# Four reorderings in a two-layer linear-attention and MLP kernel: rows before stores, output weights written later, a third tile turned earlier, statistics a tile ahead

## The chip, the core and the metric

The kernel runs on one core of one Trainium2 chip. Its engines work beside each other: TensorE (PE; loads of its weights are listed as PEld) multiplies matrices into PSUM, VectorE (DVE), ScalarE (ACT) and GpSimd (POOL) do what lies between, and SyncE (SP; its DMA queue is shown as SPq) asks for nearly all transfers between HBM and SBUF. The metric is device microseconds (us) of one execution. Before the change it is 2492.43 us, the median of three runs (2491.26 to 2493.83).

## What is computed

Two layers, each a Hedgehog linear attention (A) and an MLP with squared ReLU (B), all in float32, on 2048 rows of 576 numbers; there are 32 heads of 18 and 4608 hidden features.

```python
x = x + A(layernorm(x)); x = x + B(layernorm(x))      # twice, same weights
# A: q, k, v = heads(x @ wqkv)
#    phi(u) = concat(softmax(u @ w_phi), softmax(-u @ w_phi))
#    kv = phi_k^T v, z = sum over rows of phi_k
#    o  = (phi_q kv) / (phi_q z + 1e-6);  return merged(o) @ wo
# B: h = relu(x @ w1 + b1); return (h * h) @ w2 + b2
```

The sums kv and z run over all rows, so no row of a layer's attention output is known before every row's keys and values have been summed. This point is called the barrier.

## The kernel before

**Tiles.** The 2048 rows are four blocks of 512 (`NB`, `TB`); a block is four tiles of 128 rows (`NT`). The 576 columns are four chunks of 128 and a rest of 64 (`KC`, `NC` = 5). The turned features of a block come in five groups of heads (`NG`) in two halves of the feature map, so `2 * NG` = 10 steps. To keep precision, an operand of a matmul is split into a high part (ScalarE copies it) and a low part (VectorE or GpSimd subtracts), and a product is the sum of three: high by high, low by high, high by low. Weights once split are stored in HBM (`keep_split`, the stores at L406) and later loaded ready-made (L406 again).

**Order of work.** Layer 0 goes through the blocks in the order [3, 2, 0, 1], layer 1 in [1, 0, 3, 2]. In a layer: the barrier, with the attention output of order[0] (`g_out` with two parts and `pause`); the MLP of order[0] (`g_mlp`), into which the attention of order[1] is woven (`back_first`); the MLP of order[1], into which the attention of order[2] and order[3] is woven (`back_second`); then the MLP of the last two blocks as a pair (`g_pair`: `products` computes both blocks' hidden features and the first block's sums, `seconds` the second block's sums). Into layer 0's `seconds` the norms, values and keys of layer 1 are woven (`back_keys`).

**Who sets the order.** Python generators write the instructions down in one order: `weave(main, other, rate)` lets the other generator advance by the costs it yields, `pipeline` staggers stages over tiles. A scheduler then orders each engine's queue when the program is built: among what is ready by its own model, that which was written earlier goes first, unless `tc.issue_after` holds it behind a named instruction. Each engine, SyncE too, runs its queue strictly in that order, so an instruction that waits holds up all behind it. A load can be placed long before the place where it was written, if its buffer slot is free.

**The places that are touched.**
- The barrier, `g_out` with `pause`: the block's last two row tiles need their features scaled first: `product` (L828), `total` (sums, L831), `factors` (L797 to L800), `rescale` (L805), for halves 0 (VectorE) and 1 (GpSimd) of tiles 2 and 3. `between` writes them behind the first part's last eviction, with two `o_add` (L939), which add the first output products to the rows that `rows_in` loaded (L922). TensorE's transposes at L888 wait for the rescaled halves. `pieces` loads and splits the output weights, with GpSimd's low parts at L384.
- Without `behind`, in the blocks of order[2] and order[3], `pieces` loads the stored output weights: eight loads (L406), four of 567 KB and four of 81 KB.
- `last`, at the end of order[0]'s attention: transposes (L480, L494) and splits (ScalarE L488 and L501, VectorE L489 and L502) of the normalized tiles 2 and 3. `g_mlp` runs it (`drain(rest)`) behind the first half products (L1121) of its first two groups of features. A group's weights are loaded at L1091, L1093 and L238 and split at L1099 to L1106.
- `last_rows(0)` in `g_pair`: the last products are added to the rows of xm, in their last 128 columns at L1492, in the others at L1496, and the sum is stored to xs (L1498).
- `back_keys` and `g_norm` with `fine`: `start` loads a tile (L1742) and takes its statistics (L438, L441 on VectorE, L442 and L443 on GpSimd), `apart` normalizes it (L469, L470), `cross` transposes, `split` splits. The tag "x" has five slots, for the rows of `last_rows` and those of the norm.

Of the kernel before, what the change touches and what calls it, by code (L numbers as in the profile page):

```python
# [15 lines left out]
NT = TB // P  # L16
# [5 lines left out]
def layers_kernel(  # L22
# [18 lines left out]
    nc = tc.nc  # L41
# [10 lines left out]
    NC = KC + 1  # L52
    HG = P // DH
    GW = HG * DH
    NG = (H + HG - 1) // HG
# [24 lines left out]
    kept = set()  # L80
# [6 lines left out]
    spare = {"tags": [], "i": 0}  # L87
# [9 lines left out]
    def drain(gen):  # L97
        for _ in gen:
            pass
# [13 lines left out]
    def pipeline(n, stages, costs):  # L113

        for i in range(n + len(stages) - 1):
            for k in reversed(range(len(stages))):
                if 0 <= i - k < n:
                    stages[k](i - k)
                    yield costs[k]
# [36 lines left out]
    def lagged(n, produce, consume, by=1):  # L156

        held = {}
        for i in range(n + by):
            if i < n:  # L160
                held[i] = produce(i)
            if i >= by:
                consume(i - by, held.pop(i - by))
            if i < n or i == n + by - 1:
                yield
# [54 lines left out]
    dense = {"v": 0}  # L220
# [200 lines left out]
    def keep_split(which, pair):  # L421
        if which not in kept:
            for half in range(2):
                moved(which, half, pair[half], True)
            kept.add(which)
# [26 lines left out]
    def g_norm(x_of, dst, name, then=None, fine=False):  # L452
# [69 lines left out]
        xns, pts, begun = {}, {}, {}  # L522
# [16 lines left out]
            else:  # L539
                split_main(i // 3 * 2 + i % 3, pts.pop(i))  # L540

        yield from pipeline(NT, (start, apart), (2.0, 1.6))
        yield from pipeline(3 * NT // 2, (cross, split), (0.3, 0.9))

    def spill(b, x):
# [312 lines left out]
    def g_out(layer, b, ph, dst, name, parts=1, pause=None, behind=None, norm=None, mid=None, costs=(None, None)):  # L858
# [51 lines left out]
        def pieces():  # L910
            with ExitStack() as order:
                for ins in behind or ():
                    order.enter_context(tc.issue_after(ins.ins))
                if not pause or "o" in kept:
                    return wpair("o", name, low=nc.gpsimd if parts > 1 else None)
                two = [wpiece(wo, 0, f"{name}o0", heads=True, low=nc.gpsimd)]
            with tc.issue_after(late_products().ins):
                return two + [wpiece(wo, HP, f"{name}o1", heads=True, low=nc.gpsimd)]

        def rows_in(t):  # L920
            x = sb.tile([P, D], F32, tag="x", name=f"{name}x{t}", bufs=5)
            nc.sync.dma_start(x, x_in[b * TB + t * P : b * TB + (t + 1) * P] if layer == 0 else xs[b][t])  # L922
            return x
# [23 lines left out]
        if pause:  # L947
            product, total, factors, rescale = pause()
            with tc.issue_after(dense["scaled0"].ins):
                product(2, 0)  # L950
                total(2, 0)
        pair = pieces() if behind or "o" in kept else None
        if pair:
            keep_split("o", pair)
        if pause and not late:
            late_products()
        xs_of = []
        yield

        def between(pts):  # L960
            steps = [lambda: product(3, 0), lambda: total(2, 1), lambda: factors(2), lambda: rescale(2, 1),
                     lambda: total(3, 0), lambda: total(3, 1), lambda: factors(3), lambda: rescale(3, 1),
                     lambda: o_add(xs_of[0], pts[0], 0), lambda: o_add(xs_of[1], pts[1], 0),
                     lambda: rescale(2, 0), lambda: rescale(3, 0)]
            for step in steps:
                step()
                yield

        for part in range(parts):
            if pause and part:  # L970
                xs_of += [rows_in(t) for t in range(2)]
                pts = [o_product(t, half) for half in range(2) for t in range(2)]
                with tc.issue_after(dense["part"].ins):
                    drain(chained(between(pts), every=True))
            for i, _ in enumerate(lagged(2 * NG, lambda i: turn(part, i), lambda i, f: times(part, i, f), parts)):
                if pause and part and i in (1, 2):
                    with tc.issue_after(dense["turned"].ins):
                        o_add(xs_of[i - 1], pts[1 + i], 1)
                yield costs[0]
# [3 lines left out]
        pair = pair or pieces()  # L983
# [10 lines left out]
        begin, scale, main, rest = next(g_norm(xs_of.__getitem__, dst, f"{name}n", None, None))  # L994
        owns, xns, ox = {}, {}, {}
# [68 lines left out]

        def last():
            spare.update(tags=[f"acc{i}" for i in range(NC)], i=NC + 1)
            pts = [main[0](t, xns[t]) for t in (2, 3)]
            pts.append(rest[0](1))
            spare["tags"] = []
            yield  # L1070
            main[1](2, pts[0])
            main[1](3, pts[1])
            rest[1](1, pts[2])
            yield

        dense["rest"] = last()
# [2 lines left out]
    def g_mlp(layer, b, x, after, name, rest=None, then=None):  # L1079
# [3 lines left out]
        R = D - P  # L1083
# [76 lines left out]
        for f in range(2):  # L1160
            first(f, rest is not None)
            with tc.issue_after(traced_on(nc.tensor)) if rest else nullcontext():
                hidden(f, halves[0])
        if rest:
            with tc.issue_after(dense["hidden"].ins):
                drain(rest)
        acc += [ps_a.tile([P, TB], F32, tag=f"acc{c}", name=f"{name}acc{c}") for c in range(NC)]
        for low in lows:
            with tc.issue_after(dense["normed"].ins), tc.issue_after(dense["lowered"].ins):
# [187 lines left out]
    def g_pair(layer, blocks, x, after, name):  # L1357
# [120 lines left out]
        def last_rows(b):  # L1478
            f = (b + 1) * NF - 1
            features(f, range(3))  # L1480
            yt = sb.tile([P, TB], F32, tag="hr", name=f"{name}yt{b}", bufs=2)
            nc.scalar.activation(yt, accs[b][KC], AF.Copy)
            by_rows(f, range(2), range(3))
            pt = ps_w.tile([P, TB], F32, tag="w", name=f"{name}py{b}")
            p3 = pt.rearrange("p (t d) -> p t d", d=P)
            for t in range(NT):
                nc.tensor.transpose(p3[:, t], yt[:, t * P : (t + 1) * P], ident)
            xs_ = after if b else []
            for t in range(NT):
                xr = sb.tile([P, D], F32, tag="x", name=f"{name}x{b}{t}", bufs=5)  # L1490
                nc.sync.dma_start(xr, xm[blocks[b]][t])
                nc.vector.tensor_add(xr[:, R:], p3[:, t], xr[:, R:])  # L1492
                xs_.append(xr)
            by_rows(f, range(2, NT), range(3))
            for t, xr in enumerate(xs_):
                dense["added"] = nc.vector.tensor_add(xr[:, :R], accs[b][t][:, :R], xr[:, :R])  # L1496
                at = blocks[b] * TB + t * P
                nc.sync.dma_start(out[at : at + P] if layer else xs[blocks[b]][t], xr)  # L1498
            del high[f], wide[f]
# [221 lines left out]
    for layer in range(2):  # L1721
# [101 lines left out]
        for k, _ in enumerate(products):  # L1823
            if k == NP - 1:
                with tc.issue_after(dense["paired"].ins):
                    for _ in range(2):
                        next(back, None)
        with tc.issue_after(dense["added"].ins):
            for _ in range(4):
                next(back, None)  # L1830
        weave(seconds, back, 0.85)
        if layer == 0:

# [33 lines left out]
```

## Time and profile before

| | us |
|---|---|
| runs, median (lowest to highest) | 2492.43 (2491.26 to 2493.83) |
| profiled execution | 2491.15 |
| its span, first to last instruction | 2489.2 |
| TensorE busy | 2463.1 |
| VectorE busy | 1535.0 |
| ScalarE busy | 1263.0 |
| GpSimd busy | 956.7 |
| largest wait of TensorE (t0opt, L888) | 3.1 |

The clock granted to TensorE was 0.999 of full speed over the span. Tile names tell the place: t0 and t1 are the barriers of layers 0 and 1, a_2, a_0 and so on the attention of a block, m_3 and so on the MLP of a block, m_p the pair, n_3 a block's norm in `back_keys`, w_3v its value weights. In rows of the timeline the columns are the start in us, the length in us, the engine, line and operation, the tile written and the tiles read, shapes, the count of like instructions merged, and in brackets the idle time before with what ended it. Instructions of one engine overlap a little, so that lengths are somewhat above the distance between starts.

### The profile page before, as it was taken

To read this page: it belongs to the slowest core of one execution; us is meant where nothing else is said; L and a number is where in the kernel's file an instruction comes from. 1 tells how busy PE (TensorE), PEld (TensorE's weight loads), DVE (VectorE), ACT (ScalarE), POOL (GpSimd) and SP (SyncE) were. 2 spreads that over 40 slices of the span, in tenths; PEclk is the share of its full clock that TensorE was granted. 3 is DMA by queue.
4 is the path that set the end of the run, shared out by engine and by line. 5 is a ranking of instruction groups with operands and counts; after the bars stand their busy time and mean duration, and the time that the engine had idled before them with its cause. 6 is when DMAs were issued, how large, how long until landed. Compare 5 with 4: busy or idle time off the path is not lost. (4 is left out here: it accounts for less than half of the span.)

```text
span 2489.2 us, 41471 instructions
## 1 busy us (share of the span) xinstructions
PE 2463.1 (99%) x15108; PEld 2169.4 (87%) x15108; DVE 1535.0 (62%) x2507; ACT 1263.0 (51%) x2243; POOL 956.7 (38%) x1101
## 2 busy tenths in 40 slices
PE   8999999999999999999999999999999999999999
PEld 8998888889888888888999988888888888888888
DVE  7778938454756655545756787584557665454454
ACT  4344545443546766664443445554445466666543
POOL 4445303212335565541433442132122355565322
PEclk9999999999999999999999999999999999999999
DMA  9124533346434433338754144334473444333363
GB/s 332 60 71 146 169 105 94 103 156 224 131 120 134 146 104 105 110 100 287 250 196 144 54 169 116 103 99 117 153 243 96 125 136 139 115 104 112 108 200 127
DMA packets 248892, 348.67 MB, mean 140 GB/s; under 512 B 30127, under 2 KB 155951, under 8 KB 246127
## 3 DMA queue, kind: packets, MB, share of 16 engines
q1 hardware_dynamic: 247428, 344.66, 44.0%
q8 instruction: 118, 1.93, 0.3%
q10 hardware_dynamic: 1258, 1.37, 0.2%
q14 instruction: 88, 0.71, 0.1%
HBM read 280.93 MB, written 65.00 MB: 139 GB/s over the span
## 5 line engine op out<-in xcount | busy, mean ns | idle before, releaser
L1428 POOL TENSOR_TENSOR m_ps<-m_pr,m_ps 128x128 fp32r<-128x128 f32 x144 | 118.2, 821 | 310.9 <-ACT m_ps L1426 248.7
L1427 DVE TENSOR_TENSOR m_ps<-m_pr,m_ps 128x448 fp32r<-128x448 f32 x144 | 97.9, 680 | 166.1 <-ACT m_ps L1426 162.6
L1470 PE MATMUL m_pacc<-m_ps,m_phb 128*128 128x448 f32 x864 | 188.5, 366 | 0.0
L1470 PEld LDWEIGHTS m_pacc<-m_ps,m_phb 128*128 128x128 f32 x864 | 162.1, 188 | 18.2
L1426 ACT ACTIVATE m_ps<-m_pr 128x576 fp32r<-128x576 f32 x144 | 98.4, 683 | 128.1 <-issue 71.5
L1470 PE MATMUL m_pacacc<-m_ps,m_phc 128*128 128x448 f32 x648 | 150.3, 368 | 0.7 <-DVE m_px L1496 0.7
L1470 PEld LDWEIGHTS m_pacacc<-m_ps,m_phc 128*128 128x128 f32 x648 | 119.2, 188 | 10.0 <-DVE m_px L1496 1.0
L1148 PE MATMUL m_0acc<-m_0s,m_0hb 128*128 128x448 f32 x432 | 100.2, 366 | 0.0
L1148 PE MATMUL m_2acc<-m_2s,m_2hb 128*128 128x448 f32 x432 | 100.2, 366 | 0.0
L1148 PE MATMUL m_3acc<-m_3s,m_3hb 128*128 128x448 f32 x432 | 99.7, 365 | 0.0
L1148 PE MATMUL m_1acc<-m_1s,m_1hb 128*128 128x448 f32 x432 | 99.7, 365 | 0.0
L1121 PE MATMUL m_3ph<-t0onh,m_3h 128*128 128x512 f32 (+1 forms) x380 | 97.6, 382 | 0.6 <-ACT t0onh L488 0.5
L1121 PE MATMUL m_1ph<-t1onh,m_1h 128*128 128x512 f32 (+1 forms) x380 | 97.5, 382 | 0.6 <-ACT t1onh L488 0.5
L1121 PE MATMUL m_2ph<-a_2nh,m_2h 128*128 128x512 f32 (+1 forms) x380 | 97.7, 384 | 0.0
L1121 PE MATMUL m_0ph<-a_0nh,m_0h 128*128 128x512 f32 (+1 forms) x380 | 97.6, 384 | 0.0
L1148 PEld LDWEIGHTS m_2acc<-m_2s,m_2hb 128*128 128x128 f32 x432 | 80.9, 188 | 10.6 <-ACT m_2hb L1129 0.2
L1148 PEld LDWEIGHTS m_0acc<-m_0s,m_0hb 128*128 128x128 f32 x432 | 80.9, 188 | 10.6 <-ACT m_0hb L1129 0.2
L1148 PEld LDWEIGHTS m_1acc<-m_1s,m_1hb 128*128 128x128 f32 x432 | 81.1, 188 | 10.3
L1148 PEld LDWEIGHTS m_3acc<-m_3s,m_3hb 128*128 128x128 f32 x432 | 81.1, 188 | 10.3
L1106 POOL TENSOR_TENSOR m_3s<-m_3r,m_3s 128x128 fp32r<-128x128 f32 x36 | 24.6, 684 | 161.6 <-ACT m_3s L1100 148.1
L1106 POOL TENSOR_TENSOR m_1s<-m_1r,m_1s 128x128 fp32r<-128x128 f32 x36 | 24.2, 673 | 162.2 <-ACT m_1s L1100 154.8
L1106 POOL TENSOR_TENSOR m_0s<-m_0r,m_0s 128x128 fp32r<-128x128 f32 x36 | 28.1, 779 | 138.8 <-ACT m_0s L1100 131.1
(2439 smaller groups left out, 7341.3 us busy)
## 6 DMA issues: line engine op xcount, KB each, us to landing
m_pr<-in_B_w SPq DMA_DIRECT2D x144, 288.0 KB
m_pr<-in_B_w SPq DMA_DIRECT2D x72, 256.0 KB
hd<-m_pu SPq DMA_DIRECT2D x72, 256.0 KB
m_pg<-hd SPq DMA_DIRECT2D x72, 256.0 KB
m_3r<-in_B_w SPq DMA_DIRECT2D x36, 288.0 KB
m_2r<-in_B_w SPq DMA_DIRECT2D x36, 288.0 KB
m_1r<-in_B_w SPq DMA_DIRECT2D x36, 288.0 KB
m_0r<-in_B_w SPq DMA_DIRECT2D x36, 288.0 KB
```

The source lines that it names most:

```text
L1106: nc.gpsimd.tensor_sub(s2[:, D + R : 2 * D], r2[:, R:], s2[:, R:D].bitcast(F32))
L1121: dense["hidden"] = nc.tensor.matmul(ph[:, cols], a, m, start=(k == 0), stop=(k == len(ops) - 1))
L1148: nc.tensor.matmul(acc[t][:, :R], a[:, rows], m, start=(f == 0 and k == 0), stop=(f == NF - 1 and k == 2))
L1426: nc.scalar.activation(s2[:, :D], r2, AF.Copy)
L1427: nc.vector.tensor_sub(s2[:, D : D + R], r2[:, :R], s2[:, :R].bitcast(F32))
L1428: nc.gpsimd.tensor_sub(s2[:, D + R : 2 * D], r2[:, R:], s2[:, R:D].bitcast(F32))
L1470: nc.tensor.matmul(accs[b][t][:, :R], a[:, rows], m, start=(g == 0 and k == 0), stop=(g == NF - 1 and k == 2))
```

## The change

It has four edits, and adds or removes no arithmetic and no transfer.

1. In the barrier the first two row loads are written ahead of the stores of the split output weights (`keep_split("o", pair)`); before, these stores stood first and the rows were written at the start of the second part. The steps of `between` are reordered: `total(2, 1)`, `factors(2)` and `rescale(2, 1)` ahead of `product(3, 0)`, which was first.
2. In blocks without `behind` the output weights are loaded when half of the turned features are written (`i == NG`) instead of ahead of them all.
3. `last` is two steps: transposes and splits of tile 2, written behind the first half product of feature group 0, and those of tile 3 and of the rest, behind that of group 1. Before, both tiles and the rest were one step of transposes and one of splits, behind both half products.
4. In `g_norm` with `fine` a tile's statistics are written one tile ahead of the normalization of the one before. `back_keys` is advanced by one step, not two, behind the last product of the pair, and by one, not four, behind the adds of `last_rows(0)`. In `last_rows(0)` the four small adds (L1492) stand behind the four large ones.

```diff
@@ g_norm, fine
-        yield from pipeline(NT, (start, apart), (2.0, 1.6))
+        start(0)
+        yield 2.0
+        for t in range(NT):
+            if t + 1 < NT:
+                start(t + 1)
+                yield 2.0
+            apart(t)
+            yield 1.6
         yield from pipeline(3 * NT // 2, (cross, split), (0.3, 0.9))
@@ g_out
-        pair = pieces() if behind or "o" in kept else None
-        if pair:
-            keep_split("o", pair)
+        pair = pieces() if behind else None
         if pause and not late:
             late_products()
         xs_of = []
+        if pause:
+            xs_of += [rows_in(t) for t in range(2)]
+            keep_split("o", pair)
         yield
         def between(pts):
-            steps = [lambda: product(3, 0), lambda: total(2, 1), lambda: factors(2), lambda: rescale(2, 1),
+            steps = [lambda: total(2, 1), lambda: factors(2), lambda: rescale(2, 1), lambda: product(3, 0),
                      lambda: total(3, 0), lambda: total(3, 1), lambda: factors(3), lambda: rescale(3, 1),
...
             if pause and part:
-                xs_of += [rows_in(t) for t in range(2)]
                 pts = [o_product(t, half) for half in range(2) for t in range(2)]
...
             for i, _ in enumerate(lagged(2 * NG, lambda i: turn(part, i), lambda i, f: times(part, i, f), parts)):
+                if not behind and i == NG:
+                    pair = pieces()
@@ last
             spare.update(tags=[f"acc{i}" for i in range(NC)], i=NC + 1)
-            pts = [main[0](t, xns[t]) for t in (2, 3)]
-            pts.append(rest[0](1))
+            pt = main[0](2, xns[2])
             spare["tags"] = []
-            yield
-            main[1](2, pts[0])
-            main[1](3, pts[1])
-            rest[1](1, pts[2])
+            main[1](2, pt)
+            yield
+            spare.update(tags=[f"acc{i}" for i in range(NC)], i=NC + 2)
+            pt, pr = main[0](3, xns[3]), rest[0](1)
+            spare["tags"] = []
+            main[1](3, pt)
+            rest[1](1, pr)
             yield
@@ g_mlp, in the loop over the first two groups
-        if rest:
-            with tc.issue_after(dense["hidden"].ins):
-                drain(rest)
+            if rest:
+                with tc.issue_after(dense["hidden"].ins):
+                    next(rest)
@@ last_rows
-                nc.vector.tensor_add(xr[:, R:], p3[:, t], xr[:, R:])
+                if b:
+                    nc.vector.tensor_add(xr[:, R:], p3[:, t], xr[:, R:])
...
                 dense["added"] = nc.vector.tensor_add(xr[:, :R], accs[b][t][:, :R], xr[:, :R])
+            for t, xr in enumerate(xs_):
+                if not b:
+                    with tc.issue_after(dense["added"].ins):
+                        nc.vector.tensor_add(xr[:, R:], p3[:, t], xr[:, R:])
@@ layers_kernel
                 with tc.issue_after(dense["paired"].ins):
-                    for _ in range(2):
-                        next(back, None)
+                    next(back, None)
         with tc.issue_after(dense["added"].ins):
-            for _ in range(4):
-                next(back, None)
+            next(back, None)
```

## The prediction

> **What bounds the kernel now.** I read the profile page first for the span and the busy shares, then the table of waits of TensorE, longest first, then the timeline around each wait that a changed line can touch.
>
> ```profile
> span 2489.2 us, 41471 instructions
> PE 2463.1 (99%) x15108; PEld 2169.4 (87%) x15108; DVE 1535.0 (62%) x2507; ACT 1263.0 (51%) x2243; POOL 956.7 (38%) x1101
> ```
>
> TensorE is busy for 2463.1 of 2489.2 us. No matmul is added or removed, so the most that any reordering can win is the idle 26.1 us, 1% of the span; a loss has no such ceiling, since every wait put in front of TensorE adds to the end. The columns of the next rows are who waits, for whom, total us, times, longest.
>
> ```profile
> PE t0opt L888 <- DVE t0fQ2e L805: 3.1, 1, 3.1
> ...
> PE n_3p L494 <- DVE n_3l L489: 1.9, 1, 1.9
> PE a_3pn L904 <- DVE a_3fl L891: 1.8, 1, 1.8
> ...
> PE a_0pn L904 <- DVE a_0fl L891: 1.2, 1, 1.2
> PE m_pach L1470 <- DVE m_ps L1427: 0.9, 1, 0.9
> PE m_pacacc L1470 <- DVE m_px L1496: 0.7, 1, 0.7
> ```
>
> These six waits, 9.6 us together, are what the diff can reach: the barrier (3.1), the attention blocks of the second pair (1.2 in layer 0, 1.8 in layer 1), and the start of layer 1's norms (0.7, 0.9, 1.9). The profiled run took 2491.15 us, 1.95 outside the span, and lies 1.28 under the median of the runs, 2492.43. The sum below is made in us of the span and then taken from the median. About 0.2%, 5.0 us, is what a measurement of this kernel can tell from no change.
>
> **Part 1, rows ahead of the weights' stores, and the barrier's order.** VectorE in layer 0's barrier, then SyncE's queue, then GpSimd:
>
> ```profile
> 209.00 1.98 DVE L828 TENSOR_TENSOR t0fm<-t0fQ3e,zb 128x576 f32<-128x576 f32 x1
> ...
> 215.00 0.23 DVE L800 TENSOR_TENSOR t0fQ3r<-t0fQ3r,t0fu 128x64 f32<-128x64 f32 x1
> 216.16 0.46 DVE L939 TENSOR_TENSOR t0ox<-t0opo,t0ox 128x288 f32<-128x288 f32 x1 [0.94 <-DMA t0ox<-in_A_x]
> 217.71 0.46 DVE L939 TENSOR_TENSOR t0ox<-t0opo,t0ox 128x288 f32<-128x288 f32 x1 [1.09 <-DMA t0ox<-in_A_x]
> 218.09 0.75 DVE L805 TENSOR_TENSOR t0fQ2e<-t0fQ2e,t0fQ2r 128x576 f32<-128x576 f32 x1
> ```
>
> ```profile
> 210.38 1.57 SPq L406 DMA_DIRECT2D wsol<-t0oo1l  x2
> 212.04 1.78 SPq L922 DMA_DIRECT2D t0ox<-in_A_x  x4
> ```
>
> ```profile
> 207.67 3.96 POOL L384 TENSOR_TENSOR t0oo1l<-t0oo1r,t0oo1h 126x1152 fp32r<-126x1152 f32 x2
> ...
> 215.37 1.16 POOL L805 TENSOR_TENSOR t0fQ3e<-t0fQ3e,t0fQ3r 128x576 f32<-128x576 f32 x1 [1.29 <-DMA t0ox<-in_A_x]
> ```
>
> The last rescaling that TensorE waits for ends at 218.84. In front of it VectorE stands idle twice for the block's rows, 0.94 and 1.09 us, because SyncE asks for them at 212.04, behind stores (210.38) that wait for GpSimd's splits of 207.67. After the edit the rows are asked for ahead of those stores and are there by 215.23, when the factors end. Both gaps go, 2.03 us. What is late next is the rescaling itself: its start moves from 218.09 to 216.06, and there GpSimd still runs its own rescaling (215.37 to 216.53). Layer 1, which stores no weights, shows that order already:
>
> ```profile
> 1442.72 1.41 DVE L831 TENSOR_REDUCE t1fu<-t1fm 128x32 f32<-128x576 f32 x2
> ...
> 1445.91 1.56 DVE L805 TENSOR_TENSOR t1fQ2e<-t1fQ2e,t1fQ2r 128x576 f32<-128x576 f32 x1
> ```
>
> ```profile
> 1442.94 1.17 POOL L805 TENSOR_TENSOR t1fQ2e<-t1fQ2e,t1fQ2r 128x576 f32<-128x576 f32 x1 [7.35 <-DVE t1fQ2r L800]
> 1445.69 1.17 POOL L805 TENSOR_TENSOR t1fQ3e<-t1fQ3e,t1fQ3r 128x576 f32<-128x576 f32 x1 [1.58 <-DVE t1fQ3r L800]
> ```
>
> There the same rescaling took 1.56 instead of 0.75 beside GpSimd's. So 216.06 + 1.56 = 217.62 against 218.84: I take a gain of 1.2, of a possible 2.03, and at least 0. The product that moves behind the factors (1.98 beside the split) is the same work on the same engine; in layer 1 nothing in front of it is late, so I cost the reorder at 0. It could cost 1.17 in each layer, if it had to sit out GpSimd's rescaling of 1442.94, which then starts just ahead of it. I take 0 because the instruction behind the factors starts at 1442.72, before GpSimd's at 1442.94.
>
> The Trainium skill ("SBUF — State Buffer", section "Who interferes with whom") says that a VectorE instruction with two SBUF inputs and a GpSimd instruction that reads SBUF hold a shared port exclusively, whoever starts first. It speaks against the reorder, which puts two such instructions side by side; 1.56 against 0.75 agrees, and by it the sum would come out between the one above and 2.3 us less gain, according to who starts first.
>
> **Part 2, the output weights.** The eight loads of these weights are written behind the first half of the turned features in the blocks of order[2] and order[3]. SyncE's queue and ScalarE in layer 0, then the chain of waits in layer 1 (start, us, what), then the first use of these weights:
>
> ```profile
> 519.36 0.79 SPq L406 DMA_DIRECT2D a_0o1l<-wsol  x1
> 520.24 1.07 SPq L1093 DMA_DIRECT2D m_2r<-in_B_w  x2
> ...
> 523.87 0.40 SPq L922 DMA_DIRECT2D a_0x<-in_A_x  x1
> ```
>
> ```profile
> 525.97 0.69 ACT L1100 ACTIVATE m_2s<-m_2r 128x576 fp32r<-128x576 f32 x1 [2.10 <-DMA m_2r<-in_B_w]
> ```
>
> ```profile
> 1747.20 0.73 SPq L406
> ...
> 1748.03 6.36 DMA m_0r<-in_B_w
> ```
>
> ```profile
> 551.17 0.30 PE L933 MATMUL a_0po<-a_0o0h,a_0oh 126*128 126x288 f32 x1
> ```
>
> The MLP's weights are asked for at 520.24, behind the last piece of the output weights (519.36), and ScalarE's split of them (525.97, after a wait of 2.10) stands in front of the eviction for which TensorE waits 1.2. In layer 1 the same piece costs the queue 0.83 (1747.20 to 1748.03) before a transfer of 6.36. The pieces issued earlier found their slots free and the queue idle, and SyncE hoists such loads (at 523.87 it asks for a_0's rows, 27 us before the products of 551.17 that they are added to). So I expect the early pieces to stay and only the last to fall behind: 0.88 (520.24 less 519.36) plus its share of the transfers, about 0.35, covers the 1.2 of layer 0; and 0.83 + 0.35 = 1.2 of the 1.8 in layer 1. Together 2.4, with 0 and 3.0 as bounds. The weights then have until 551.17; order[3]'s have longer.
>
> **Part 3, the third tile turned sooner.** TensorE, then VectorE, as the MLP of order[0] starts:
>
> ```profile
> 236.53 0.85 PE L1121 MATMUL m_3ph<-t0onh,m_3h 128*128 128x256 f32 x5
> ...
> 239.95 1.04 PE L480 MATMUL t0onp<-ident,t0onn 128*128 128x128 f32 x8
> ...
> 241.72 1.68 PE L1121 MATMUL m_3ph<-t0onh,m_3h 128*128 128x256 f32 x9 [0.52 <-ACT t0onh L488]
> ```
>
> ```profile
> 238.09 0.49 DVE L469 TENSOR_SCALAR t0onn<-t0ox,t0onm,t0ond 128x512 f32<-128x512 f32 x1
> ...
> 242.54 0.43 DVE L502 TENSOR_TENSOR t0onh<-t0onp,t0onh 64x256 fp32r<-64x256 f32 x1
> ```
>
> Two half products take 3.42 us (236.53 to 239.95), 1.71 each. The third tile's transposes now follow the first, at 238.24; their input is ready at 238.58, so TensorE waits about 0.4 with the second half product queued behind. Its own eviction is then covered, but the fourth tile's transposes come some 0.4 later and the 0.52 wait behind them shrinks by about 0.3. Net loss 0.1 per layer, 0.2 in all, between a loss of 0.9 (the 0.4 not recovered) and a gain of 1.0 (the 0.52 gone in both).
>
> **Part 4, layer 0's last rows, and part 5, statistics a tile ahead.** VectorE, its waits between 1100 and 1170, SyncE's queue, and the DMA rows of 1143.5 to 1147.2:
>
> ```profile
> 1139.30 0.87 DVE L1492 TENSOR_TENSOR m_px<-m_ppy,m_px 128x128 f32<-128x128 f32 x4
> 1140.09 1.14 DVE L1496 TENSOR_TENSOR m_px<-m_pacc,m_px 128x448 f32<-128x448 f32 x2
> ...
> 1142.21 0.61 DVE L1427 TENSOR_TENSOR m_ps<-m_pr,m_ps 128x448 fp32r<-128x448 f32 x1
> ```
>
> ```profile
> DVE n_3n L469 <- POOL n_3d L443: 3.8, 4, 1.0
> ```
>
> ```profile
> 1142.41 1.13 SPq L1742 DMA_DIRECT2D x<-xs  x2
> ```
>
> ```profile
> DMA packets 437, 1.13 MB, mean 306 GB/s; under 512 B 48, under 2 KB 48, under 8 KB 436
> ...
> w_3v0h<-wsvh SPq DMA_DIRECT2D x1, 720.0 KB
> ```
>
> The four small adds (0.79 from start to start) move behind the two large ones, which free the accumulators 0.79 sooner: the 0.7 wait goes, gain 0.7 (0 to 0.8). The split of 1142.21 stands behind a tile's statistics that had waited for a load; with fewer steps of the norm forced ahead it no longer does: gain 0.8 of its 0.9 (0 to 0.9). The price: the next tile's row took the slot that the first tile's normalization freed. With statistics a tile ahead it needs a slot whose store has landed, as the loads of 1142.41 do, and that store is issued 0.79 later. I cost this at 0: the normalizations no longer each wait about 1.0 for GpSimd's root (3.8 in four), which pays back some 3 us of a load that has to wait for a store, and the transposes are written further down, behind more of the second products. The 1.9 wait at n_3p stays; bounds, it goes (gain 1.9) or grows as in rival A.
>
> The Trainium skill ("DMA: Bandwidth & Descriptors", section "Anatomy of one DMA") gives about 2.0 us plus bytes over 436 GB/s for a DMA. A store and a load of one row tile (128 x 576 numbers, 288 KB) would by it take an estimated 5.4 us, whatever lies before them; the rows here show a transfer of the same size at 6.36 behind others. No term of the sum rests on it.
>
> **Sum:** -1.2 - 2.4 + 0.2 - 0.7 - 0.8 = -4.9 us. The profiled time would be 2486.2, the median 2487.5.
>
> **The rivals.**
> A (can end on the other side): the late row. If the three loads of 720 KB of the value weights get ahead of the last row, 2.2 MB at the 306 GB/s of that stretch are 7 us more for n_3p to wait: -4.9 + 7 = +2.1. Where the 3 us of the roots' waits aren't won back either and the store's 0.79 counts, it is 10.8 and +5.9; it decides from 9.9 on. For it: 1142.41 is already behind a store. Against it: those weights are written behind the norm's sixth step.
> B (slower): the output weights arrive late. 576 x 576 numbers in a high and a low part are 2592 KB, at 306 GB/s 8.7 us, the first half 4.4; asked for later than 546.8, TensorE waits us for us in both layers. It decides from 551.8 on, where 2 x 5.0 eat the 4.9 and 5 more. Against it: the hoisting above.
> C: all loads really move, the rescaling starts clear of GpSimd, and n_3p's wait goes: -4.9 - 0.6 - 0.8 - 1.9 = -8.2.
> D: the loads and the rows keep their places: -4.9 + 1.2 + 2.4 = -1.3.
> E: the product loses to GpSimd's rescaling in both barriers: -4.9 + 2.3 = -2.6. That is the port rule's case.
>
> **How the numbers follow.** Forecast 0.40 (own range -7 to -2; faster by over 0.2% in 0.22, within it in 0.18), A 0.19 (within 0.09, slower 0.10), B 0.08 (slower), C 0.22 (faster), D 0.06 and E 0.05 (within). Faster 0.44, within 0.2% 0.38, slower 0.18. The range from -10.4 (2482) to +4.1 (2496.5) leaves out B, the worst of A and a little beyond C.
>
> **What would show it.** Right: no gap before the two adds of L939 in layer 0's barrier and t0opt's wait near 1.9; the load of L1093 ahead of the last a_0o1l and a_3o1l, and the waits of a_0pn and a_3pn gone and near 0.6; m_pacacc's and m_pach's waits gone; m_3ph's two waits about 0.6 together. Wrong: a row of L1742 landing after the value weights and n_3p's wait above 4; a_0po or a_3po in the table of waits; a new wait of 1 us or more anywhere else, since each such wait outweighs one term.

## The result, and the profile after

The changed kernel takes 2486.89 us, the median of 11 runs (2483.94 to 2488.61), against 2491.26 for the kernel before in the same comparison (11 runs, 2488.80 to 2493.83). The ratio is 0.9979, with a 95% interval from 0.9971 to 0.9988: 4.4 us between the two medians. A few executions of the experiments below took from 7% to several times longer, and their medians and ratios leave these out. The profiled execution took 2485.02, and its page begins:

```profile
span 2483.3 us, 41469 instructions
...
PE 2462.7 (99%) x15108; PEld 2169.3 (87%) x15108; DVE 1533.3 (62%) x2507; ACT 1262.7 (51%) x2243; POOL 959.9 (39%) x1101
```

TensorE's work is the same, 15108 matmuls; the span is 5.9 us shorter. So the difference lies in waits and pace, not in work. The table of TensorE's waits after the change (who, for whom, total us, times, longest; lines are some 7 to 16 higher than before):

```profile
PE k_3kp L571 <- DMA w_3k1l<-wskl: 1.5, 1, 1.5
PE t0opt L895 <- DVE t0fQ2e L812: 1.2, 1, 1.2
PE n_3p L480 <- DVE n_3n L469: 1.1, 1, 1.1
PE n_3p L494 <- DVE n_3l L489: 0.9, 2, 0.7
```

Gone altogether are a_0pn (1.2), a_3pn (1.8), m_pach (0.9) and m_pacacc (0.7); t0opt fell by 1.9. The norm n_3 waits 2.0 in three places instead of 1.9 in one. New is k_3kp: TensorE stands 1.5 us for the last piece of the key weights. Together -6.5 + 0.1 + 1.5 = -4.9 in the table; of the rest of the 5.9, 0.5 is the first wait for DMA (fp, 2.5 before and 2.0 here), which reads 2.0 to 3.3 in the profiles of this study.

Waits are not all that TensorE loses. Behind the wait of t0opt the kernel before ran on at a lower granted clock. The four microseconds from TensorE's restart, here and in the kernel with the rows and the barrier changed alone (below); the columns are the stretch, its length, the busy us and the number of instructions of PE, PEld, DVE, ACT and POOL, the granted clock, the DMA share and GB/s:

```profile
218.90:222.90 4.00, 3.72 (x19) 3.27 (x20) 2.75 (x7) 1.95 (x6) 0.62 (x1) 0.68 0.03 8
```

```profile
218.30:222.30 4.00, 3.68 (x25) 3.00 (x26) 3.16 (x9) 2.99 (x8) 0.96 (x1) 1.00 0.01 4
```

The clock record of the kernel before reads 0.5 for 3.41 us from 220.3 on. From the restart to the last product of the barrier the same matmuls take 17.2 to 17.5 us in the seven profiles that have such a stretch there, and 16.3 to 16.4 in the seven without: 1.1 us that count as busy and stand in no row of waits.

**The barrier.** VectorE, then SyncE's queue, after the change:

```profile
209.12 0.64 DVE L804 TENSOR_TENSOR t0fu<-t0fu,t0fQ2r 128x64 f32<-128x64 f32 x1
209.80 0.70 DVE L805 SCALAR_TENSOR_TENSOR t0fu<-t0fu 128x32 f32<-128x32 f32 x1
...
211.06 0.75 DVE L835 TENSOR_TENSOR t0fm<-t0fQ3e,zb 128x576 f32<-128x576 f32 x1
...
214.31 0.82 DVE L946 TENSOR_TENSOR t0ox<-t0opo,t0ox 128x288 f32<-128x288 f32 x2
215.04 1.27 DVE L812 TENSOR_TENSOR t0fQ2e<-t0fQ2e,t0fQ2r 128x576 f32<-128x576 f32 x1
```

```profile
203.94 1.27 SPq L929 DMA_DIRECT2D t0ox<-in_A_x  x2
```

The rows are asked for at 203.94, and the two adds follow the factors without a gap. The rescaling now takes 1.27 instead of 0.75: it stands beside GpSimd's, as forecast. The product takes 0.75 instead of 1.98, since GpSimd's split is over (at 210.44) when it comes; the small factors in front of it pay part of that (0.64 and 0.70, against 0.23 and 0.19 before). The product starts 0.23 us ahead of GpSimd's rescaling (211.06 against 211.29, and in layer 1 1438.00 against 1438.23), keeps its 0.75 in both layers, and GpSimd's takes 1.55 instead of 1.17.

**The output weights.** SyncE's queue in layer 0:

```profile
511.35 0.36 SPq L1104 DMA_DIRECT2D m_2r<-in_B_w  x1
511.75 1.21 SPq L406 DMA_DIRECT2D a_0o1h<-wsoh  x1
514.32 2.42 SPq L1215 DMA_DIRECT2D xs<-m_3x  x4
516.84 0.91 SPq L1104 DMA_DIRECT2D m_2r<-in_B_w  x1
517.81 0.69 SPq L406 DMA_DIRECT2D a_0o1h<-wsoh  x1
518.54 0.84 SPq L406 DMA_DIRECT2D a_0o1l<-wsol  x2
```

Five of the eight pieces keep their early places (up to 511.75), three fall behind. The two loads of the MLP's weights that were asked for together at 520.24 now go at 511.35 and 516.84, the first of them ahead of the stores of 514.32 as well. ScalarE's split, which stood at 525.97 and waited for its DMA, is at 522.31 and does not:

```profile
522.31 0.69 ACT L1111 ACTIVATE m_2s<-m_2r 128x576 fp32r<-128x576 f32 x1 [0.81 <-issue]
```

**The norm and its weights.** After the change SyncE asks for the value weights earlier and for the rows later:

```profile
1134.64 0.43 SPq L406 DMA_DIRECT2D w_3v1l<-wsvl  x1
1136.48 2.82 SPq L1514 DMA_DIRECT2D xs<-m_px  x4
1142.27 1.68 SPq L1758 DMA_DIRECT2D x<-xs  x3
```

The stores of 1136.48 go out behind 720 KB of value weights, and the row loads, which need the slots of the stored tiles, come 5.8 us after the first of them (2.8 in the kernel before, 1139.60 to 1142.41).

### The profile page after: what moved, and what is told of

It is laid out like the page before. It is cut to its first block, busy times and chain, and to the rows that moved or that the text cites. A ratio compares the mean times of both kernels' runs of the same rounds, so it can differ in the third digit from the quotient of the medians.

```text
span 2483.3 us, 41469 instructions
## 1 busy us (share of the span) xinstructions
PE 2462.7 (99%) x15108; PEld 2169.3 (87%) x15108; DVE 1533.3 (62%) x2507; ACT 1262.7 (51%) x2243; POOL 959.9 (39%) x1101
## 4 chain that ended last, share of the span: by engine, by line
PE 94%; DVE 3%; DMA 1%; issue 1%; ACT 0%; POOL 0%; SPq 0%; DVEq 0%; ACTq 0%; POOLq 0%
PE m_ppx L1449 9%; PE m_pacc L1481 7%; PE m_ppy L1449 5%; PE m_1ph L1132 5%; PE m_3ph L1132 5%; PE m_0ph L1132 5%; PE m_2ph L1132 5%; PE m_pacacc L1481 4%; PE m_2acc L1159 4%; PE m_0acc L1159 4%; PE m_1acc L1159 3%; PE m_3acc L1159 3%; PE m_ppz L1449 2%; PE m_pacc L1471 2%; PE m_pacacc L1471 2%; PE m_pach L1481 1%
## 5 line engine op out<-in xcount | busy, mean ns | idle before, releaser
L1159 PEld LDWEIGHTS m_2acc<-m_2s,m_2hb 128*128 128x128 f32 x432 | 80.9, 188 | 10.6 <-ACT m_2hb L1140 0.2
L1159 PEld LDWEIGHTS m_0acc<-m_0s,m_0hb 128*128 128x128 f32 x432 | 80.9, 188 | 10.6 <-ACT m_0hb L1140 0.2
L1132 PEld LDWEIGHTS m_3ph<-t0onh,m_3h 128*128 128x128 f32 x380 | 68.8, 188 | 14.0 <-ACT t0onh L488 0.7
```

The costliest lines, as they stand in the source:

```text
L1132: dense["hidden"] = nc.tensor.matmul(ph[:, cols], a, m, start=(k == 0), stop=(k == len(ops) - 1))
L1159: nc.tensor.matmul(acc[t][:, :R], a[:, rows], m, start=(f == 0 and k == 0), stop=(f == NF - 1 and k == 2))
```

## The experiments

All ratios are to the kernel before, run on the same chip beside the experiment. Differences of 1 or 2 us lie near what the runs can tell, so the waits of each profile were read as well. Each kernel was profiled once.

### Rows and barrier alone

The kernel before with the rows ahead of the stores and the new order of steps.

```diff
-        if pair:
+        if pair and not pause:
             keep_split("o", pair)
...
+        if pause:
+            xs_of += [rows_in(t) for t in range(2)]
+            keep_split("o", pair)
...
-            steps = [lambda: product(3, 0), lambda: total(2, 1), lambda: factors(2), lambda: rescale(2, 1),
+            steps = [lambda: total(2, 1), lambda: factors(2), lambda: rescale(2, 1), lambda: product(3, 0),
...
-                xs_of += [rows_in(t) for t in range(2)]
```

> The kernel before with part 1 alone: the two row loads written ahead of the stores of the split output weights, and the new order of the barrier's steps. If the rows were what held the barrier (the prediction's reason), both idle stretches before the adds at L939 go and the wait of t0opt falls from 3.1 to 1.9 (the prediction's term, with the rescaling held up beside GpSimd) or to the 1.2 seen with all edits; the rest of the trace keeps its waits, so the time falls by 1.2 to 2.2 us. Rival: the barrier of the changed kernel is shorter through the order of the steps, or through what the other edits moved; then t0opt stays near 3 here.

Ratio 0.9991 (0.9981 to 1.0001), medians 2488.53 against 2490.89; the interval just takes in no change, so the wait is what shows the effect. TensorE's waits:

```profile
PE t0opt L888 <- DVE t0fQ2e L805: 1.2, 1, 1.2
PE a_0pn L904 <- DVE a_0fl L891: 1.2, 1, 1.2
PE a_3pn L904 <- DVE a_3fl L891: 1.1, 1, 1.1
```

t0opt falls to the 1.2 of the changed kernel, so part 1 does it alone; the rival that other edits did it falls. (The order of the steps is taken by itself below.) But a_3pn, which nothing in this kernel touches, reads 1.1 where the profile of before had 1.8.

### Output weights alone

```diff
-        pair = pieces() if behind or "o" in kept else None
+        pair = pieces() if behind else None
...
+                if not behind and i == NG:
+                    pair = pieces()
```

> The kernel before with part 2 alone: the output weights written behind half of the turned features. The prediction's reason: the early pieces keep their place in SyncE's queue and only the late ones fall behind the MLP's weights; then the waits of a_0pn (1.2) and a_3pn (1.8) fall by 1.2 each, to about 0 and 0.6, and the time by 2.4. By the trace of the changed kernel both go whole, 3.0 in the table of waits and 3.3 from start to start. Rival: the loads move as a whole to where they are written; then the first of them is asked for only some 18 us after the place of the kernel before. Other rival: part 2 did nothing and the two waits went through other edits; then both stay.

Ratio 0.9987 (0.9978 to 0.9997), 2488.22 against 2490.89. Neither a_0pn nor a_3pn is in the table of waits any more. Here, too, an untouched wait differs from its value in the profile of before:

```profile
PE t0opt L888 <- DVE t0fQ2e L805: 2.3, 1, 2.3
```

### Statistics alone

The statistics a tile ahead and one forced step at both places; the small adds as before.

```diff
-        yield from pipeline(NT, (start, apart), (2.0, 1.6))
+        start(0)
+        yield 2.0
+        for t in range(NT):
+            if t + 1 < NT:
+                start(t + 1)
+                yield 2.0
+            apart(t)
+            yield 1.6
...
-                    for _ in range(2):
-                        next(back, None)
+                    next(back, None)
...
-            for _ in range(4):
-                next(back, None)
+            next(back, None)
```

> The kernel before with the statistics a tile ahead and fewer steps forced (without the move of the small adds). The prediction: the 0.9 wait of m_pach goes, the 1.9 of n_3p stays, so -0.8. From the trace of the changed kernel: m_pach's wait goes, n_3p waits about 2.0 in three places, and the key weights make a new wait at k_3kp of 1.5, so about +0.5 to +1. Rival: k_3kp's wait comes from another edit; then -0.8 and no wait at k_3kp.

Ratio 1.0007 (0.9997 to 1.0016), 2492.28 against 2490.89.

```profile
PE k_3kp L571 <- DMA w_3k1l<-wskl: 2.4, 1, 2.4
...
PE n_3p L480 <- DVE n_3n L469: 1.1, 1, 1.1
PE n_3p L494 <- DVE n_3l L489: 0.8, 2, 0.6
...
PE k_3kp L571 <- DMA w_3k1h<-wskh: 0.7, 1, 0.7
```

Both m_pach and m_pacacc are gone, without the move of the small adds, and k_3kp makes 3.1 us of new waits; behind them the granted clock reads 0.5 for 6.83 us. The new wait belongs to this edit.

### Small adds alone

```diff
-                nc.vector.tensor_add(xr[:, R:], p3[:, t], xr[:, R:])
+                if b:
+                    nc.vector.tensor_add(xr[:, R:], p3[:, t], xr[:, R:])
...
+            for t, xr in enumerate(xs_):
+                if not b:
+                    with tc.issue_after(dense["added"].ins):
+                        nc.vector.tensor_add(xr[:, R:], p3[:, t], xr[:, R:])
```

> The kernel before with the four small adds behind the large ones in layer 0's last rows, nothing else. The prediction: the wait of m_pacacc (0.7) goes and nothing else, -0.7. Rival: the split at L1427 then stands behind more work and m_pach's wait of 0.9 grows by what m_pacacc's falls, so that the time stays.

Ratio 1.0012 (1.0002 to 1.0021), 2493.73 against 2490.89: alone this is a loss, just clear of noise.

```profile
PE n_3p L494 <- DVE n_3l L489: 3.1, 1, 3.1
...
PE a_0pn L904 <- DVE a_0fl L891: 2.4, 1, 2.4
...
PE m_pach L1470 <- DVE m_phc L1520: 1.0, 1, 1.0
```

The wait of m_pacacc goes, but m_pach waits 1.3 (these 1.0 and 0.3 for m_ps) instead of 0.9, and n_3p 1.2 longer. The rival holds in part: on VectorE the small adds (1144.69) now stand in front of the next tile's statistics (1145.48) and of the operand m_phc that m_pach waits for (1146.21). The whole loss is not theirs: a_0pn's 2.4, twice the value before, is again a wait that the edit does not touch, and the clock reads 0.5 for 3.41 us both behind it and behind n_3p's wait.

### Fewer forced steps alone

The kernel before with one forced step at both places (the last two blocks of the diff under "Statistics alone").

> The kernel before with only the number of forced steps changed (one and one, not two and four), the statistics not ahead and the small adds in their old place. It tells apart what in part 5 does what. If the fewer steps clear VectorE for the adds and the split, the waits of m_pacacc and m_pach go here too, and if they move the value weights' loads ahead of the rows, k_3kp's wait comes here too (1.5 to 3). If the statistics a tile ahead do it, the waits stay as before.

Ratio 1.0011 (1.0002 to 1.0021), 2493.36 against 2491.14.

```profile
PE n_3p L494 <- DVE n_3l L489: 2.7, 1, 2.7
...
PE n_3p L480 <- DVE n_3n L469: 0.9, 1, 0.9
PE m_pach L1470 <- DVE m_phc L1515: 0.7, 1, 0.7
...
PE k_3kp L564 <- DMA w_3k1l<-wskl: 0.3, 1, 0.3
```

Fewer steps clear m_pacacc and leave 0.7 of m_pach, and n_3p waits 3.6: without the statistics ahead each later tile still waits for its root. VectorE's waits for the root are 2.5 in three here, and 0.5 in one in the changed kernel. So m_pach needs both halves of the edit. k_3kp's wait is there in small (with another 0.2), so the fewer steps alone bring its cause. The reverse, the statistics ahead with the old number of steps, was not run: two rows of the norm and the four of last_rows would have to be held at once, in five slots.

### Without the statistics

The changed kernel with the statistics and steps of before.

> The changed kernel with the statistics and the forced steps of the norm as before; rows, output weights, third tile and small adds stay changed. The two runs before it say: the statistics' edit removes the waits of m_pach and m_pacacc and makes the one at k_3kp; the small adds alone move their wait to m_pach and n_3p. Then here k_3kp's wait is gone, m_pach waits about 1.3 and n_3p about 3, and the time is 0 to 2.5 us above the changed kernel. Rival: the statistics' edit is a loss as a whole (it read +1.3 of 2491 alone); then this kernel is faster than the changed one by 1 or more.

Ratio 0.9988 (0.9978 to 0.9997), 2487.51 against 2491.09.

```profile
PE n_3p L494 <- DVE n_3l L489: 2.9, 1, 2.9
...
PE m_pach L1474 <- DVE m_phc L1524: 1.2, 1, 1.2
...
PE m_pach L1474 <- DVE m_ps L1431: 0.3, 1, 0.3
```

As expected, 4.4 us of waits here against 3.5 (1.5 + 1.1 + 0.9) in the changed kernel. So on top of the small adds the statistics' edit is worth about 0.9 by the waits and 0.8 by the medians (-3.6 here, -4.4 for the whole change), which the intervals cannot tell from nothing. Rows alone (-2.4) and output weights alone (-2.7) already add up to about -5 by their medians, against -4.4: nothing measurable is left for parts 3 to 5 together.

### The old order of the barrier's steps

The changed kernel with product(3, 0) first again, the rows still early.

> The changed kernel with the steps of the barrier in the order of before (product(3, 0) first), the rows still ahead of the stores. If the rows alone shorten the barrier (the prediction costs the reorder at 0), t0opt waits 1.2 here too. If the reorder is what avoids the wait beside GpSimd's split (the product took 1.98 there before), the product is long again and t0opt waits some 0.6 to 1.2 more.

Ratio 0.9986 (0.9976 to 0.9995), 2486.91 against 2491.14. A row of the timeline and two of the waits:

```profile
209.11 1.93 DVE L835 TENSOR_TENSOR t0fm<-t0fQ3e,zb 128x576 f32<-128x576 f32 x1
```

```profile
PE t0opt L895 <- DVE t0fQ2e L812: 1.4, 1, 1.4
...
PE k_3kp L571 <- DMA w_3k1l<-wskl: 0.5, 1, 0.5
```

The product is long again, and t0opt waits 0.2 more. The rows carry the gain; the reorder is worth 0.2, by one profile against 1.2 in all eight with the new order.

### Without the third tile's move

The changed kernel with `last` in its old form.

> The changed kernel with the third tile turned together with the fourth, as before. The prediction's term is a loss of 0.1 per layer, so 0.2 us faster than the changed kernel; by the starts of the matmuls in the two traces the edit is even in layer 0 and gains 0.1 in layer 1. Rival: the earlier tile was worth more than that and the waits at m_3ph and m_1ph grow by over 0.5 each.

Ratio 0.9985 (0.9976 to 0.9994), 2487.31 against 2491.14.

The two waits at m_3ph and m_1ph read 0.5 each, as in the changed kernel and the one before. The starts tell more. From the last product of the barrier (t0opo) to the first of a_0's queries (a_0qp) TensorE runs the same 67 matmuls in every kernel. Before, then after:

```profile
236.41 0.29 PE L933 MATMUL t0opo<-t0oo1h,t0oolt 72*128 72x288 f32 x1
...
245.50 0.42 PE L564 MATMUL a_0qp<-a_0q0h,a_0uh 128*128 128x288 f32 x2
```

```profile
233.70 0.29 PE L940 MATMUL t0opo<-t0oo1h,t0oolt 72*128 72x288 f32 x1
...
243.01 0.42 PE L571 MATMUL a_0qp<-a_0q0h,a_0uh 128*128 128x288 f32 x2
```

That is 9.1 us against 9.3. The seven kernels with the old `last`, this one among them, take 9.06 to 9.12, the seven with the new one 9.31 to 9.36; in layer 1 it is 9.00 to 9.02 and 9.08 to 9.12. So the edit loses some 0.3 us in all, too little for the medians.

### The query weights held back

Why does k_3kp wait? Behind the key weights' last piece SyncE asks for 1.4 MB of the next barrier's query weights. Here they are held behind all SyncE work written before them; no other instruction changes its place.

```diff
-            drain(g_k(x, kpair, kes, "k1_last", ready=lambda: qpair.extend(wpair("q", "t1", TAGS_B))))
+            def late_q():
+                with tc.issue_after(traced_on(nc.sync)):
+                    qpair.extend(wpair("q", "t1", TAGS_B))
+
+            drain(g_k(x, kpair, kes, "k1_last", ready=late_q))
```

> The changed kernel with the six loads of the next barrier's query weights (t1q0r, t1q1r, 1.4 MB) held behind all SyncE work written before them; no other instruction changes its place. Theory: k_3kp's wait of 1.5 comes from these loads, which run beside the last piece of the key weights (720 KB in 3.3 us, where the kernel before took 1.8). Then that piece lands at about 1188 or before, the wait falls to 0 to 0.3, and the time by 1.2 to 1.5 us. Rival: the key weights are asked for too late by themselves, behind three row loads; then the wait stays at 1 or more. Other risk: the query weights come too late for their split; then a new wait at t1q0qp.

Ratio 0.9982 (0.9973 to 0.9991), 2486.63 against 2491.09.

```profile
PE k_3kp L571 <- DMA w_3k1l<-wskl: 1.1, 1, 1.1
```

The theory falls: 1.1 stays. With nothing behind it in the queue, the piece still landed at 1188.63, 8.75 us after it was asked for (1179.88); in the changed kernel it is 8.74 (1180.63 to 1189.37). The wait is 0.4 shorter, but the load was not faster, and kernels with the same order and the query weights in place read 0.5 and 0.6 as well as 1.5.

### Six slots for the rows, and both

The changed kernel with `bufs=6` for the tag "x" (one of eight places is shown); the second kernel also holds the query weights back.

```diff
-            x = sb.tile([P, D], F32, tag="x", name=f"{name}x{t}", bufs=5)
+            x = sb.tile([P, D], F32, tag="x", name=f"{name}x{t}", bufs=6)
```

> The changed kernel with six slots instead of five for the row tiles. Theory of the prediction's part 5: the second tile's row has no slot until a store of last_rows(0) has landed (load at 1142.27, store landed at 1142.20), and that holds n_3p for about 2.0 us. With a sixth slot the load goes before the stores, some 5 us earlier, and n_3p's waits fall to under 1; the time falls by 1 to 2. Rival: the loads then meet the 720 KB pieces of the value weights in the queue, and n_3p's waits stay near 2. Elsewhere more rows can be asked for early, which can move other loads.

> Both: six slots for the rows and the query weights held back. If the two waits are independent the gains add up, 2.2 to 3.5 us below the changed kernel; if the earlier rows move the key weights in the queue, less.

Ratios 0.9977 (0.9967 to 0.9986) and 0.9978 (0.9969 to 0.9986). n_3p waits 1.6 with six slots, 1.9 with both, and k_3kp 1.8 and 1.4; the changed kernel has 2.0 and 1.5. Neither expectation was met, n_3p under 1 or gains that add up. A sixth slot alone does little: the second tile's statistics are still written behind the stores, and its load was asked for at 1138.89, 3.2 us after the first store (1135.65).

### Six slots and both statistics early

Six slots, and two forced steps behind the pair's last product, which are now both statistics.

```diff
                 with tc.issue_after(dense["paired"].ins):
-                    next(back, None)
+                    for _ in range(2):
+                        next(back, None)
```

> The changed kernel with six slots for the rows and two steps of the norm, both statistics, behind the pair's last product. The second tile's row then is asked for before the stores of last_rows(0), not behind them. If the row held n_3p, its first wait (1.1 in the changed kernel) goes and the time falls by about 1 against six slots alone. Rival: the statistics then stand ahead of the adds on VectorE again and m_pacacc's or m_pach's wait comes back at 0.5 to 1.

Ratio 0.9969 (0.9958 to 0.9980), 2482.13 against 2491.14.

```profile
PE n_3p L494 <- DVE n_3l L489: 0.6, 1, 0.6
...
PE n_3p L480 <- DVE n_3n L469: 0.5, 1, 0.5
```

n_3p waits 1.1 in all, m_pacacc and m_pach do not come back, and k_3kp is gone. The queues show why. SyncE in the changed kernel, then in this one:

```profile
1178.68 0.33 SPq L1435 DMA_DIRECT2D m_pr<-in_B_w  x1
1179.23 0.32 SPq L1524 DMA_DIRECT2D m_pg<-hd  x1
1179.97 0.32 SPq L406 DMA_DIRECT2D w_3k1h<-wskh  x1
1180.63 0.32 SPq L406 DMA_DIRECT2D w_3k1l<-wskl  x1
```

```profile
1180.21 0.32 SPq L406 DMA_DIRECT2D w_3k1h<-wskh  x1
1180.88 0.32 SPq L406 DMA_DIRECT2D w_3k1l<-wskl  x1
1181.30 0.37 SPq L1435 DMA_DIRECT2D m_pr<-in_B_w  x1
1181.76 0.63 SPq L1524 DMA_DIRECT2D m_pg<-hd  x1
```

The key weights are asked for at nearly the same time. In the changed kernel 544 KB of the pair's loads stand directly in front of them, and the last piece lands at 1189.37; here those loads stand behind, as in the kernel before, and it lands at 1186.66. All fourteen profiles agree: from issue to landing the last piece takes 5.3 to 5.8 us in the six kernels that ask for it ahead of a pair's loads, and 7.9 to 10.6 in the eight that ask for it directly behind them; in two of the eight, with the query weights held back, it is 8.75 and 8.73. So k_3kp's wait comes from the place in SyncE's queue, and the query weights have no share in it that these profiles show. Of all kernels measured this has the lowest time; its interval still overlaps that of the changed kernel.

## Why the prediction was right, and where its steps were not

The forecast was 2487.5, 4.9 us less; measured are 2486.89 and 4.4 less. A wait in one profile is one draw out of a spread, so the terms are best taken from all fourteen profiles, as the time from the start of one matmul of TensorE to the start of another, with the same matmuls between them (us; in brackets how many kernels):

| stretch of TensorE | part as before | part changed |
|---|---|---|
| layer 0's barrier, last t0q2qp to last t0opo | 34.65 to 35.60 (5) | 32.60 to 33.62 (9) |
| output weights, layer 0, first m_3py to first m_2py | 317.15 to 317.39, once 320.00 (5) | 315.92 to 316.10 (9) |
| output weights, layer 1, first m_1py to first m_0py | 316.86 to 317.96 (5) | 315.96 to 316.05 (9) |
| third tile, last t0opo to first a_0qp | 9.06 to 9.12 (7) | 9.31 to 9.36 (7) |
| third tile, last t1opo to first a_3qp | 9.00 to 9.02 (7) | 9.08 to 9.12 (7) |
| norms, first m_pach to first t1pv; parts 4 and 5 both | 242.17 to 243.35 (3) | 241.97 to 243.30 (3) |

By the averages that is -2.2 for part 1, -2.4 for part 2 (without the 320.00 of adds alone), +0.3 for part 3 and -0.2 for parts 4 and 5: -4.5 together. Term by term:

- **Part 1, -1.2.** Right in cause and order, half of the gain unseen. The two gaps before L939 went and the rescaling was held up beside GpSimd, by 0.52 (1.27 for 0.75) rather than 0.81. In the two profiles t0opt fell by 1.9, but five executions with the old barrier read 3.1, 2.3, 2.1, 2.5 and 2.6 (before, and with output weights, statistics, adds and steps alone), 2.5 on average, and every one with the early rows 1.2 or 1.4. Against that average the wait gives 1.3. The rest is pace: all five with the old barrier have the 3.41 us at half the clock behind the wait, and only two of nine with the early rows, the changed kernel of the profile being one. The prediction's ceiling, the idle 26.1 us, has no such loss in it. The reorder, costed at 0, is worth 0.2.
- **Part 2, -2.4.** Right as mechanism: early pieces stay, late ones fall behind. Three fell behind, not one, and the MLP's load took the place that a piece of the output weights had, ahead of the stores too; so both waits went whole, 3.0 in the two profiles, where 2.4 was the price of the last piece. Here too the profile of before was one draw: without the edit a_0pn read 1.2, 1.2, 1.3, 2.4 and 1.3, a_3pn 1.8, 1.1, 0.8, 0.9 and 0.7, so 2.5 for the pair on average.
- **Part 3, +0.2.** Right: 0.2 in layer 0 and 0.1 in layer 1. From the first half product to the third tile's transposes it is 2.10 us in the changed kernel (233.83 to 235.93) and 1.71 of that is the half product, so TensorE lost the 0.4 of the prediction there, though the row of waits shows 0.2.
- **Part 4, -0.7, and part 5, -0.8.** Both waits went, but not by the terms as split: the statistics' edit clears both, and the small adds alone only move their wait, at a loss.
- **What failed: "I cost this at 0".** For n_3p's row it held (2.0 against 1.9), by the two effects that were set against each other: the row came later, and the roots no longer queued. But the step looked only at n_3. Writing the norm's steps later reorders SyncE's queue for what comes after, and 40 us on the second half of the key weights fell behind two loads. This new wait at k_3kp, 1.5 in the profile and between 0.5 and 3.1 in others of the same order, is on no line of the sum; a new wait of 1 us or more was the prediction's own sign of being wrong, and it came. With it parts 4 and 5 are worth about nothing and not 1.5.

So the sum came out well by luck as well as by reason: parts 1 and 2 carry the whole gain, part 1 with a microsecond more than forecast from a clock that the sum does not know, and parts 4 and 5 with 1.3 less from a wait that it does not know. The two nearly cancel. Of the rivals, A happened in a mild form: the value weights did get in front, of the stores rather than of the rows, and the price was small. E did not come: the product started ahead of GpSimd's rescaling in both layers, as the prediction argued. The port rule of the Trainium skill ("SBUF — State Buffer", section "Who interferes with whom") fits the rows: in the new order the two-input factors took 0.64 and 0.70 beside GpSimd's split, while the reduction in front of them kept its 0.74. But it gave no loss here, since the long product got clear of the split. The fit that the prediction takes from the Trainium skill ("DMA: Bandwidth & Descriptors", section "Anatomy of one DMA") is given there for transfers that GpSimd issues; those here are SyncE's. By it 720 KB would take an estimated 3.7 us; the first key piece of the last kernel above, on an idle queue, took 4.4 (1180.21 to 1184.65).

## What to carry to other kernels

Where a kernel is 99% bound by one engine, add up the waits of that engine, look at its clock behind the long ones, and for each edit ask which of them it ends and which loads move in the queue afterwards, for as long as that queue still shows a different order. A wait that hangs on a DMA is a draw: read it from several executions, or take its term with a spread as large as itself. To price one edit, time a stretch that runs the same matmuls in both kernels, from start to start: up to the barrier, where nothing is edited, the spans of these profiles already differ by 2.6 us (200.13 to 202.70), more than any single term. Edits on one queue are not additive: the statistics (ratio 1.0007) and the small adds (1.0012), each slower alone, were together about even, and the norms got clearly shorter (238.97 in the table's last stretch, one profile) only when a sixth slot and the step that uses it came together.

## What was not expected of the hardware

**The granted clock.** In nine of the fourteen profiles it reads 0.5 for stretches of 3.41 us (twice 6.83) between the start-up and the end. After the start-up every wait of TensorE that is 2.1 us or longer has one behind it: t0opt with the old barrier, a_0pn's 2.4, n_3p's 2.6, 2.7, 2.9 and 3.1, and k_3kp's 2.4. Of the nine waits of 1.2 or 1.4 at t0opt two have one, and the 1.9 of n_3p and the 1.8 of a_3pn have none. Output weights alone has one behind the 0.7 and 0.9 of m_pacacc and m_pach. So a wait of 2 us or more cost another 1.1 us in the barrier; what decides for shorter ones is left open.

**Waits behind transfers** differ between profiles whose instructions around them are the same: t0opt from 2.1 to 3.1, a_0pn from 1.2 to 2.4, a_3pn from 0.7 to 1.8. By contrast a_2np and a_0np, which wait for VectorE's normalization, read 0.6 in every profile of this study.

**The key weights.** Two pieces of 720 KB took 6.6 us from the landing before them (1182.07) to 1188.63 with nothing behind them in SyncE's queue, some 225 GB/s, while the stretch of 1143.5 to 1147.2 in the kernel before moved 306. The trace has sixteen completions for a load: those of the last piece lie between 1185.04 and 1188.63 there, and between 1185.85 and 1186.72 in the kernel before. So it is the last of the sixteen that came late; what held it was not found.
